# Attention and FFN on one core: the first loads on two queues, and TensorE's order on batch 0 written out

## The chip, the cores and the metric

The kernel runs on one core of one Trainium2 chip. A core has five engines that work side by side, each through its own queue in order: TensorE (PE; its weight loads are shown apart as PEld), VectorE (DVE), ScalarE (ACT), GpSimd (POOL) and SyncE (SP). Transfers are issued from SP, ACT and POOL and carried out by 16 DMA engines. The metric is the device time of one execution in microseconds (us); lower is better.

## The reference

The input is q, k and v, each 8 batches x 12 heads x 448 positions x 64. Every head computes

```
scores = q k^T / 8
attn   = max(scores, 0)^2 / 448
x      = attn v
```

There is no softmax: a ReLU and a square stand in its place. The heads are laid side by side to x of 8 x 448 x 768, and then

```
xn  = (x - mean) / sqrt(var + 1e-6) * g_ln
out = x + max(xn W1, 0) W2        # W1 768 x 3072, W2 3072 x 768
```

All inputs and the output are in fp32; the kernel multiplies in bf16.

## The kernel before, in words

Work goes batch by batch. A batch's 12 heads make three blocks of four heads (`NPER = 3`), numbered n = 0, 1, 2 for batch 0, n = 3, 4, 5 for batch 1, and so on. The 448 positions are cut into 7 pieces of 64 (`J = 7`). For a block:

- `att_T` (transposes, L481) turns q and k so that the head dimension lies on partitions. TensorE transposes into PSUM, and copies (L361 on ACT, L363 on DVE; one helper `copy`, L359) put the result into `qkT`. A block has 56 transposes, 28 of q and 28 of k. From batch 2 on, DMA transposes do this.
- `att_QK(n, s)` (L559) makes the scores of one piece of k against all of q: 4 matmuls into one of three PSUM slots ("slots"). A ReLU with the scale (L568 on ACT, L570 on DVE) writes bf16 to SBUF and frees the slot; a square in place follows (L585 on DVE, L583 on ACT).
- `att_AV(n, s)` (L623) multiplies with v and sums over the seven pieces into two PSUM banks (`f_banks`, for batch 0 alone). After s = 6 the block's part of x, already turned, is copied to `xT_all`, one copy for each half.

When x of a batch is there, `mean_part` (L687, L689, batch 0 alone) or `center` sums over d_model with a matmul against a constant 1/768; DVE subtracts it (L837), ACT or DVE multiplies with g_ln (L826, L828), and the FFN starts: `ffn_1_first` (eight matmuls without a use of their result at L880, then L885) for the first three columns of 128 of W1 on batch 0, `ffn_1` (L902) for the others, evacuated with a ReLU (L918, L920), and `ffn_2` (L959), whose output is scaled and added to x on DVE (L973) and stored. While TensorE runs a batch's FFN, the attention of the next batch is put between its matmuls. 1/std is applied only at that last step, from `bn_stats` of x.

The order is set in three ways. Each engine's queue is in order. What goes onto the queues is decided when the program is built, by a planner (`Order`, L41): each operation has the engines that may do it, a cost on each, its dependencies and a key; the planner keeps a clock for each engine and always commits the operation that can start first, and for one with a choice of engines the one that would end it first. `OVER` (L47) says how much of an instruction overlaps with the next of its queue. And TensorE's pieces come from lists. For batch 0 a loop (L1191) takes from two lists, `av_stream` (transposes of blocks 1 and 2, A.V pieces, mean parts) and `qk_stream` (scores, the transposes of block 3, one score piece of block 3), whichever the planner's clocks let start first. Later `greedy` (L1106, batch 1) and `segment` (L1068) mix FFN and attention in the same manner.

The first loads are written apart (`load_first`, L337): q and k of block 0 come in fp32 through SP's queue, in three transfers (`FIRST`, L335: q whole, k's columns 0 to 2, k's columns 3 to 6), and each is cast to bf16 by DVE or ACT. All others are cast by the DMA itself and issued from POOL (`load`, L316), at most eight in flight, in the order of lines 1163 to 1177: block 1, v, block 2, block 3, then W1 in parts among the rest of batch 1, then W2. The first transposes take the pieces of `FIRST` one by one: q and k's first three columns, then (`att_T(0, 1)`) k's last four; the scores of s < 3 need only the first two pieces.

The copies of block 3's transposes (L523, `pn == 0`, one for q and one for k) are put to the planner as soon as their transposes are. `held_relu` holds back the ReLU of block 3's first score until batch 0's x is copied out (L571 to L579).

Of the kernel before, what the change touches and what calls it, by code (L numbers as in the profile page):

```python
# [40 lines left out]
class Order:  # L41
# [5 lines left out]
    OVER = {"PE": 0.0, "ACT": 80.0, "DVE": 80.0, "POOL": 0.0, "SP": 0.0}  # L47
# [152 lines left out]
def kernel(  # L200
# [31 lines left out]
    N_FILL = 8  # L232
    N_O = 2
# [57 lines left out]
    nc.scalar.activation(warm, eps_sb, Act.Sqrt)  # L291
# [43 lines left out]
    FIRST = ((0, 0, J), (1, 0, 3), (1, 3, J))  # L335

    def load_first():  # L337

        raw = {}
        ops["qk_ld", 0, 0] = []  # L340
        for i, (t, j0, j1) in enumerate(FIRST):
            cols = slice(j0 * D, j1 * D)

            def emit(eng, i=i, t=t, cols=cols):
                if i == 0:
                    stage[0] = big(STAGE[0], None, t=2, r=H // 2, c=S)
                    f = big_pool.tile([P, BIG // 2], fp32, tag=TURNED[1])
                    raw[0] = f[:, :4 * S].rearrange("p (t r c) -> p t r c", t=2, r=2)
                rows = (q, k)[t][0].rearrange("h (p j) d -> (h p) (j d)", j=J).rearrange(
                    "(pr r) c -> r pr c", r=P)  # L350
                nc.sync.dma_start(raw[0][:, t, :, cols], rows[:, 0::NPER, cols])
            ld = R.add("SP", 480.0, emit, [], key=float(i), load=(2 * P, (55.0, 43.0, 110.0)[i]))

            def cast(eng, t=t, cols=cols):
                copy(eng, stage[0][:, t, 0::NPER, cols], raw[0][:, t, :, cols])
            ops["qk_ld", 0, 0].append(
                R.add(("DVE", "ACT"), (100.0 + 67.0 * (j1 - j0), 200.0 + 107.0 * (j1 - j0)), cast, [ld], key=-3.0))
# [107 lines left out]

    def at_use(last):
        at_ring.pop(0)
        at_ring.append(last)
# [3 lines left out]
    def att_T(n, part=0):  # L472
# [17 lines left out]
        if b == 0:  # L490
            evs = ops.setdefault(("T", n), [])
            pieces = list(enumerate(FIRST if n == 0 else ((0, 0, J), (1, 0, J))))
            for i, (t, j0, j1) in pieces[2 * part:2 * part + 2]:
# [26 lines left out]
        if pn == 0:  # L520
            ev = None
            for t in range(2):
                ev = R.add(("DVE", "ACT"), (620.0, 940.0), lambda eng, t=t: copy(  # L523
                    eng, qkT[b][:, t, pn::NPER, :], st[0][:, t].rearrange("p (j c) -> p j c", c=P)), [op, ev], key=0.01 * n - 0.008)
# [6 lines left out]
    def qk_dep(n, s):  # L531
        b, pn = divmod(n, NPER)
        if ("T", n) in ops:
            if n == 0 and s >= FIRST[1][2]:
                return ops["T", n] if len(ops["T", n]) > 2 else None
            return ops["T", n][:2]
# [724 lines left out]
```

## Time and profile before

| What | Value |
|---|---|
| Five runs | 541.92 to 542.89 us, median 542.13 |
| The profiled execution | 542.89 us, of which the span from first to last instruction is 541.03 |
| TensorE busy | 527.7 us, 98% of the span |
| VectorE, ScalarE, GpSimd busy | 285.3, 228.6, 112.6 us |
| TensorE idle before its first instruction | 5.01 us |
| First score matmul, first ReLU, first square | 6.86, 7.50, 8.44 us |
| Last square of batch 0 ends; first FFN matmul (L885) | 26.12; 30.04 us |
| Moved by DMA | 51.83 MB, mean 96 GB/s; about 200 GB/s in the first 60 us |

Times in a view count from the span's start. In the timeline a line gives the start, the busy time of a run of equal instructions, the engine, the source line, the operation and its tiles; in brackets is the idle time before it and what ended it. Instructions of one engine overlap: the next starts before the record of the last ends, so what an operation costs in a full queue is the distance between starts, not its duration. The view of waits gives, for an engine and line, what it waited for, with total, times and longest. The chain of waits follows back from the last instruction what released each step. "PE" times are partly modelled, since matmuls are pipelined.

### The profile page before, as it was taken

Reading aid. Unit: us, or ns where it says so; the run is one execution under the profiler, and the core shown is the slowest. Engines: PE = TensorE matmul, PEld = TensorE weight load, DVE = VectorE, ACT = ScalarE, POOL = GpSimd, SP = SyncE. Lnnn points to the kernel's source line nnn. Section 1 sums busy time; section 2 is a strip of 40 time slices with the busy share of each in tenths; the row PEclk is TensorE's granted clock in tenths of the full one; section 3 lists DMA queues with packets and bytes.
Section 4 is the critical chain, followed back from the end, with each engine's and each line's share of the span. In section 5 each row is a group of like instructions: output and inputs, shape, how many; then the busy total and the mean of one; then the engine's idle time right before and its main releaser. Section 6 shows DMA issues by size and latency. Waiting matters only on the chain.

```text
span 541.0 us, 9859 instructions
## 1 busy us (share of the span) xinstructions
PE 527.7 (98%) x4200; PEld 285.3 (53%) x4200; DVE 285.3 (53%) x486; ACT 228.6 (42%) x376; POOL 112.6 (21%) x129
## 2 busy tenths in 40 slices
PE   4899999999999999999999999999999999999996
PEld 3444455555554455555555455554555555555564
DVE  5979647238764566835366446752456535530011
ACT  5977612125325642556124653265422654144200
POOL 6410600131360124311061121600220102100000
PEclk9999999999999999999999999999999999999999
DMA  9999999996299104980189502993023100510022
GB/s 196 196 190 192 206 171 162 170 133 132 70 159 157 34 1 90 193 119 1 31 107 187 95 1 48 162 150 43 2 59 74 29 1 1 99 48 1 1 58 59
DMA packets 141400, 51.83 MB, mean 96 GB/s; under 512 B 121254, under 2 KB 137132, under 8 KB 141356
## 3 DMA queue, kind: packets, MB, share of 16 engines
q0 software_dynamic: 81072, 25.50, 43.8%
q1 hardware_dynamic: 55804, 14.88, 19.8%
q10 hardware_dynamic: 4480, 10.82, 7.2%
q8 instruction: 33, 0.54, 0.4%
q14 instruction: 11, 0.09, 0.1%
HBM read 51.91 MB, written 11.01 MB: 116 GB/s over the span
## 4 chain that ended last, share of the span: by engine, by line
PE 95%; DVE 2%; DMA 2%; POOL 1%; ACT 0%; issue 0%; POOLq 0%; DVEq 0%
PE o_ps L959 41%; PE ps L902 40%; PE sc L559 6%; PE ps L623 6%; DMA v_t<-in_v_dram 2%; DVE a L585 1%; PE ps L885 1%; PE ps L481 0%; DVE a L570 0%; ACT a L568 0%; POOL t L331 0%; PE ps L689 0%; PE slot L798 0%; DVE t L363 0%; ACT a L826 0%
## 5 line engine op out<-in xcount | busy, mean ns | idle before, releaser
L902 PE MATMUL ps<-a,w 128*128 128x448 bf16 x1134 | 220.4, 353 | 0.0
L959 PE MATMUL o_ps<-w,h 128*128 128x384 bf16 x1200 | 199.7, 326 | 0.0
L902 PEld LDWEIGHTS <-w 128*128 128x128 bf16 x1134 | 108.3, 98 | 108.5 <-issue 10.8
L959 PEld LDWEIGHTS <-h 128*128 128x128 bf16 x1200 | 116.1, 98 | 81.5 <-issue 5.5
L918 ACT ACTIVATE h<-ps 128x448 bf16<-128x448 f32 (+1 forms) x162 | 85.2, 527 | 104.3 <-PE ps L902 102.7
L568 ACT ACTIVATE a<-sc 128x896 bf16<-128x896 f32 x101 | 89.6, 922 | 85.9 <-PE sc L559 82.1
L570 DVE TENSOR_SCALAR a<-sc 128x896 bf16<-128x896 f32 x58 | 63.0, 1087 | 103.6 <-PE sc L559 103.5
L585 DVE TENSOR_TENSOR a<-a 128x896 bf16<-128x896 bf16 x158 | 99.3, 665 | 4.0 <-ACT a L568 3.9
L973 DVE SCALAR_TENSOR_TENSOR o_t<-o_ps,r_t,x_all 128x384 f32<-128x384 f32 x56 | 34.4, 615 | 107.4 <-PE o_ps L959 107.1
L718 POOL TENSOR_TENSOR sum_t<-sum_t,xT_all 128x384 f32<-128x384 f32 (+2 forms) x25 | 19.5, 778 | 166.7 <-ACT xT_all L361 148.1
L559 PE MATMUL sc<-t 64*64 64x448 bf16 x672 | 48.0, 361 | 2.4 <-ACT a L568 1.8
L623 PE MATMUL ps<-a,v_t 64*64 64x448 bf16 x636 | 37.4, 351 | 1.4 <-DMA v_t<-in_v_dram 0.5
L716 POOL TENSOR_TENSOR sum_t<-xT_all 128x384 f32<-128x384 bf16 (+2 forms) x13 | 10.2, 788 | 125.5 <-DVE a L585 97.2
L826 ACT ACTIVATE a<-a,g_sb 128x448 bf16<-128x448 bf16 x38 | 22.3, 656 | 25.8 <-DVE a L819 24.8
L361 ACT CAST xT_all<-ps 128x128 bf16<-128x128 f32 (+3 forms) x40 | 22.2, 560 | 25.2 <-DVE xT_all L363 13.2
L559 PEld LDWEIGHTS <-t 64*64 64x64 bf16 x672 | 17.7, 106 | 24.4 <-issue 19.1
L623 PEld LDWEIGHTS <-v_t 64*64 64x64 bf16 x672 | 19.8, 107 | 16.4 <-issue 4.6
L399 POOL DMA_DIRECT2D t<-in_q_dram x12 | 19.3, 1771 | 24.3 <-DMA t<-t 23.0
L959 PE MATMUL o_ps<-w,t 128*128 128x384 bf16 x144 | 23.9, 326 | 0.0
L399 POOL DMA_DIRECT2D t<-in_k_dram x12 | 23.7, 2525 | 0.0
L819 DVE TENSOR_TENSOR a<-xT_all,sum_t 128x768 bf16<-128x768 bf16 (+1 forms) x24 | 19.4, 852 | 6.7 <-ACT sum_t L811 6.5
L383 POOL DMA_DIRECT2D v_t<-in_v_dram x16 | 17.1, 1440 | 19.1 <-DMA w<-in_moe_w_ch_dram 17.6
(54 smaller groups left out, 187.7 us busy)
## 6 DMA issues: line engine op xcount, KB each, us to landing
out_dram<-o_t ACTq DMA_DIRECT2D x54, 192.0 KB, 2.7
v_t<-in_v_dram POOLq DMA_DIRECT2D x16, 336.0 KB, 15.5
w<-in_moe_w_ch_dram POOLq DMA_DIRECT2D x4, 1152.0 KB, 40.5
t<-in_q_dram POOLq DMA_DIRECT2D x12, 336.0 KB, 7.2
t<-in_k_dram POOLq DMA_DIRECT2D x12, 336.0 KB, 10.6
w<-in_moe_w_ch_dram POOLq DMA_DIRECT2D x4, 768.0 KB, 19.3
w<-in_moe_w_ch_dram POOLq DMA_DIRECT2D x1, 1536.0 KB, 29.3
t<-in_q_dram POOLq DMA_DIRECT2D x5, 224.0 KB, 10.2
```

Of the source, the lines that this page charges most:

```text
L361: nc.scalar.copy(o, i)
L399: nc.gpsimd.dma_start(stage[b][half * T:(half + 1) * T, t].rearrange("p j (h d) -> p j h d", d=D), src[b, half * 6:half * 6 + 6].rearrange ...
L559: nc.tensor.matmul(sc[rows_of(half), r, :S], qkT[b][rows_of(r), 1, s * NPER + pn, rows_of(half)], qT[:, :, pn, rows_of(half)], start=True, ...
L568: nc.scalar.activation(attn[n, s], st[0][:, :, :S], Act.Relu, scale=rc2)
L570: nc.vector.tensor_scalar(attn[n, s], st[0][:, :, :S], rc2, 0.0, op0=Alu.mult, op1=Alu.max)
L585: nc.vector.tensor_mul(attn[n, s], attn[n, s], attn[n, s])
L623: nc.tensor.matmul(av_st[n][half][rows_of(hh)], vt[b][rows_of(half), 2 * pn + hh, s * D:(s + 1) * D], attn[n, s][rows_of(half), hh, :], st ...
L826: nc.scalar.mul(o, o, g_sb[:, ki:ki + 1])
L902: nc.tensor.matmul(st[0], w1[:, ki, ni * P:(ni + 1) * P], xc[b][:, ki, :], start=(i == 0), stop=(i == K1 - 1))
L918: nc.scalar.activation(o, st[0][:, c], Act.Relu)
L959: nc.tensor.matmul(o_st["ps"], stat(ki), w2[:, ki, j * hd:(j + 1) * hd], start=(ki == 0), stop=(ki == K2 - 1))
L973: nc.vector.scalar_tensor_tensor(o_st[u, m][:, j * hd:(j + 1) * hd], ps, rstd[b][:, ri:ri + 1], xm[u, m][:, j * hd:(j + 1) * hd], op0=Alu. ...
```

## The change

The first k is loaded in one transfer from ACT's queue, at the same time as q in one transfer from SP's. Both are cast, transposed and copied in two pieces each (columns 0 to 3 and 4 to 6 of q, 0 to 2 and 3 to 6 of k). So that k's issue stands first on ACT, the activation that loads ACT's table (`warm`) now follows it. TensorE's order on batch 0 is a string of 49 letters, "a" for the next of `av_stream` and "q" for the next of `qk_stream`; `qk_stream` now ends with three score pieces of block 3, of which the string takes none (it has 22 q: 21 scores of batch 0 and block 3's transposes). The copies of block 3's transposes are held until batch 0's x is copied out, as the ReLU was. The planner's overlaps become 112 ns for ACT and 85 for DVE, from 80 for both, and the price of the subtraction 620 in place of 560.

```diff
-    OVER = {"PE": 0.0, "ACT": 80.0, "DVE": 80.0, "POOL": 0.0, "SP": 0.0}
+    OVER = {"PE": 0.0, "ACT": 112.0, "DVE": 85.0, "POOL": 0.0, "SP": 0.0}
...
+    FIRST_ORDER = "aqqqaqqqqqaqaqqaaaaqaqaqaqaaqqaqqqaaaqaaqaaaaaaaa"
...
-    nc.scalar.activation(warm, eps_sb, Act.Sqrt)
...
-    FIRST = ((0, 0, J), (1, 0, 3), (1, 3, J))
+    FIRST = ((0, 0, 4), (0, 4, J), (1, 0, 3), (1, 3, J))
+    LAST = len(FIRST) - 1
+    K_NEAR = FIRST[LAST][1]
 
     def load_first():
 
-        raw = {}
+        f = big_pool.tile([P, BIG // 2], fp32, tag=TURNED[1])
+        raw = f[:, :4 * S].rearrange("p (t r c) -> p t r c", t=2, r=2)
+        stage[0] = big(STAGE[0], None, t=2, r=H // 2, c=S)
+        ld = []
+        for t, src in enumerate((q, k)):
+            def emit(eng, t=t, src=src):
+                rows = src[0].rearrange("h (p j) d -> (h p) (j d)", j=J).rearrange("(pr r) c -> r pr c", r=P)
+                (nc.sync if t == 0 else nc.scalar).dma_start(raw[:, t], rows[:, 0::NPER, :])
+            ld.append(Op("SP" if t == 0 else "ACT", 480.0, emit, [], 0.0, (2 * P, 68.0)))
+            R.commit(ld[t], ld[t].engs[0], 700.0)
         ops["qk_ld", 0, 0] = []
-        for i, (t, j0, j1) in enumerate(FIRST):
+        for t, j0, j1 in FIRST:
             cols = slice(j0 * D, j1 * D)
...
-                nc.sync.dma_start(raw[0][:, t, :, cols], rows[:, 0::NPER, cols])
-            ld = R.add("SP", 480.0, emit, [], key=float(i), load=(2 * P, (55.0, 43.0, 110.0)[i]))
...
+    def wait_for_x(ev):
+
+        if ("x", NPER - 1) in ops:
+            ev.after.append(ops["x", NPER - 1])
+            R.wait.append(ev)
+        else:
+            held_relu.append(ev)
...
-            for i, (t, j0, j1) in pieces[2 * part:2 * part + 2]:
+            for i, (t, j0, j1) in pieces[LAST:] if part else pieces[:LAST if n == 0 else 2]:
...
-                ev = R.add(("DVE", "ACT"), (620.0, 940.0), lambda eng, t=t: copy(
-                    eng, qkT[b][:, t, pn::NPER, :], st[0][:, t].rearrange("p (j c) -> p j c", c=P)), [op, ev], key=0.01 * n - 0.008)
+                ev = Op(("DVE", "ACT"), (620.0, 940.0), lambda eng, t=t: copy(
+                    eng, qkT[b][:, t, pn::NPER, :], st[0][:, t].rearrange("p (j c) -> p j c", c=P)), [op, ev], 0.01 * n - 0.008)
+                wait_for_x(ev)
...
-                s1 = R.add("DVE", 560.0, sub_k, [op], key=-2.0)
+                s1 = R.add("DVE", 620.0, sub_k, [op], key=-2.0)
...
         load_first()
+        nc.scalar.activation(warm, eps_sb, Act.Sqrt)
...
-        qk_stream += [("T", NPER)] + qks(NPER, 0, 1)
+        qk_stream += [("T", NPER)] + qks(NPER, 0, 3)
         att_T(0)
         means = 0
-        while av_stream:
-            R.until(R.free["PE"])
-            tA, tQ = (start_of(piece_deps(*st[0])) if st else FAR for st in (av_stream, qk_stream))
-            if R.ahead(min(tA, tQ)):
-                continue
-            st = av_stream if tA <= tQ + 50.0 else qk_stream
-            p = st.pop(0)
+        for c in FIRST_ORDER:
+            p = (av_stream if c == "a" else qk_stream).pop(0)
             PIECE[p[0]](*p[1:])
```

On the built programs this gives: ACT has k's transfer, the table load, `warm`, the cast of q's columns 0 to 3, ten ReLUs, an x copy, seven ReLUs, an x copy, two ReLUs, an x copy, the copy of g_ln, and then one of the held copies ahead of the gains. DVE has the other three casts, the four pieces' copies, then squares; its held copy stands after its last x copy and before the subtractions. TensorE has all 56 transposes of block 0, three scores, the 56 of block 1, five scores (the fifth of block 1), and then A.V and scores in turn. Block 3's transposes stay before the end of batch 0; its first score moves behind the first FFN columns (L885). In batch 1, too, some ReLUs and squares change engine, and FFN and attention pieces alternate a little differently.

## The prediction

> **What bounds the kernel now.** I read the table of stages first, cut where TensorE's work changes kind; its columns are length, then busy time and instruction count of PE, PEld, DVE, ACT, POOL, then clock, DMA share, GB/s.
>
> ```profile
> 0.00:5.01 5.01, 0.00 (x1) 0.00 (x1) 0.91 (x4) 1.49 (x2) 4.27 (x12) 1.00 0.61 185
> 5.01:28.67 23.66, 19.57 (x405) 11.27 (x406) 20.32 (x36) 18.90 (x26) 11.74 (x17) 1.00 1.26 199
> 28.67:30.04 1.37, 1.19 (x8) 0.59 (x6) 1.37 (x3) 1.09 (x3) 0.42 (x1) 1.00 1.48 110
> 30.04:62.66 32.62, 32.62 (x386) 15.78 (x386) 25.40 (x39) 23.16 (x34) 11.13 (x10) 1.00 1.20 198
> 62.66:536.98 474.32, 474.29 (x3404) 257.65 (x3402) 236.74 (x406) 183.97 (x314) 85.02 (x93) 1.00 0.66 83
> 536.98:541.04 4.06, 0.00 (x0) 0.00 (x0) 0.62 (x1) 0.00 (x0) 0.00 (x0) 0.81 0.18 48
> ```
>
> From 30.04 us, where the first FFN matmul starts (L885), TensorE is busy to the end of its work. So the time is: start of L885, plus the TensorE work still to be done, plus a tail of 4.06. Only 30.04 us can shrink. The chain of waits from 23.5 to 31 us names what sets it:
>
> ```profile
> 24.52 1.61 DVE a L585 x3
> 26.13 0.04 issue
> 26.17 0.57 PE ps L623 x8
> 26.75 0.15 PE ps L687
> 26.90 0.86 PE ps L689 x4
> 27.76 0.31 PE sc L559 x4
> 28.07 0.50 PE ps L689 x2
> ```
>
> VectorE's squares of batch 0 (L585) come last; then the last A.V product, the evacuation of x, the mean (L689), the centering. The waits of ScalarE and VectorE from about 5 to 30 us (total, times, longest) say where they lose time:
>
> ```profile
> ACT a L568 <- PE sc L559: 2.2, 4, 0.7
> DVE t L363 <- DMA f<-in_q_dram: 3.3, 1, 3.3
> DVE a L585 <- ACT a L568: 0.4, 2, 0.2
> ```
>
> ScalarE's 2.2 us are four waits of its ReLUs for scores: 0.69 before 7.50, 0.67 before 10.70, 0.71 before 13.94, 0.16 before 28.13 (timeline of ScalarE). VectorE hardly waits: after its first square at 8.44 it is nearly full.
>
> **What the skill says.** "DMA: Bandwidth & Descriptors", Issuing engines are not separate DMA queues: transfers from several engines share 16 DMA engines and interleave, so a second issuer saves issue time alone. The trace agrees as far as it goes: q's first half megabyte moved at 360 GB/s (2.6 to 3.9 us) and k's at 343 (3.9 to 5.2), one queue at that. "TensorE: Matmul & The Clock Gate", Part 1: the first 3.4 us or so of matmuls run at half clock. Here 40 transposes took 1.28 us at 5.01 (32 ns each) and 53 took 1.01 at 16.96 (19 each); it agrees. "ScalarE: Activation LUTs", What ACT_TABLE_LOAD costs: an activation with immediates costs 186 ns + 0.833 ns an element; L361 on 448 took 0.55, the formula gives 0.56.
>
> **The change, part by part.** Prices, as distances between starts in a full queue: square 0.535 (four from 18.69 to 20.83), PSUM copy or x cast on VectorE 0.535, ReLU on VectorE 1.00 (20.83 to 21.83), ReLU on ScalarE 0.81 (six from 16.76 to 21.61), x cast there 0.415.
>
> *Loads.* Now SP issues q at 0.74 and k in two parts at 1.27 and 1.76; with 3.6, 3.6 and 3.9 us to landing they are there at 4.34, 4.9 and 5.66. After, q leaves SP and k ScalarE at about 0.74. Bytes and engines are the same, so I let both land near the end: 917 KB at the plateau of about 400 GB/s (slices of the DMA view between 2.8 and 3.6 us: 335 to 442) from 2.6 us, plus 0.4 from last data to landing (4.34 against 3.9): about 5.3. Bounds: 4.3 (two queues double the rate) and 5.7 (no gain). Behind k's issue on ScalarE stand the table load (1.28) and `warm` (0.20): from 1.2 to 2.7 us, where ScalarE has nothing else until its first cast; free. On SP only the gains' load follows, now earlier by two issues of 0.46; free. POOL's own load queue starts at about 4.6 as now.
>
> *Casts and copies in pieces.* In the built order ScalarE casts q's four columns: 186 + 0.833 x 512 = 0.61 (skill's formula; trace: none). VectorE casts k's three, k's four, q's three, 0.43 or less each, overlapped: about 1.1. TensorE then does all 56 transposes before the first score: 5.3 + 0.65 = 5.95, plus 56 x 0.032 = 1.79, makes 7.75. q's second piece is cast by 6.4, when the first 16 transposes end at 6.46; no hole. The first score now starts at 6.86: **0.89 us later**. First ReLU 8.39 (now 7.50), first square 9.34 (now 8.44). Four copies on VectorE cost 2 x 0.42 + 2 x 0.35 in place of three, all before 8.4; hidden.
>
> *The fixed list.* It puts three scores behind the first transposes, then batch 0's second transposes, then QK(0,3) to (0,6) and QK(1,0) **ahead of AV(0,0)**. Now AV stands first and blocks TensorE until v lands (wait 0.53 at 12.77), which is the 0.71 hole before 13.94; the 0.67 hole before 10.70 is the second transposes (8.40 to 10.28). With ReLUs running 8.39 to 10.9, those transposes (k landed at 9.39) end at 10.5, so the hole shrinks to about 0.1. QK(1,0) needs only a free slot at 12.9, so its ReLU starts about 13.6 (now 13.94). ScalarE has made up more than its late start.
>
> *VectorE's sum.* From the first square up to the end of the last: now 20 squares, 3 ReLUs, 4 copies, 1 x cast = 10.70 + 3.00 + 2.14 + 0.54 = 16.38 in 17.60 us (8.44 to 26.04), 1.2 of it slips, largely caused by ScalarE's holes. After, in the built order: 21 squares, 2 ReLUs, 4 copies, 2 casts = 11.24 + 2.00 + 2.14 + 1.08 = 16.46. I replayed the list: each ReLU is there before VectorE reaches its square, by 0.1 to 0.9. I take a slip of 0.4; bounds 0 and 1.2. So 9.34 + 16.46 + 0.4 = 26.20, against 26.04: a wash, late start and smoother queue.
>
> *Held copies.* The turning copies of batch 1's first block stand in VectorE's queue at 26.04, two of 0.535, ahead of the last x cast. Held until x, one goes behind that cast and one to ScalarE. QK(3,0), 0.31 in front of the last mean pair, moves behind the first FFN. Last square ends 26.28; A.V 0.05 + 0.38; x cast 26.76 to 27.38; mean 27.43 to 27.98 (0.55); subtraction 28.09 after 0.11. Now 28.67: **0.58 earlier**. On VectorE the held copy ends about 27.9, before the subtraction; on ScalarE its copy (186 + 0.833 x 896 = 0.93) ends by 28.3, before the first gain needs it at 28.7. If x slipped on ScalarE, this copy would delay the gain by up to 0.4.
>
> *The rest.* QK(3,0) comes back after L885, 4 of the 12 scores that take 0.69 there: +0.19 (bound 0.31). The other new ReLU and square placements come from the planner's overlap constants (112 and 85 in place of 80; the 0.62 squares start 0.535 apart, an overlap of 0.085); they stay under TensorE: 25.4 of 32.6 us busy on VectorE, 23.2 on ScalarE. Weight loads land as now; the built order asks for FFN column 8, the tight one (landing 42.4, used at 42.8), only after more attention, about 44.7. Sum: -0.58 + 0.19 = -0.39.
>
> The profiled execution took 542.89 us with a span of 541.03, so 1.86 outside; its new time would be 542.5. It is the slowest of the five; their median 542.13 is 0.76 lower, so I forecast **541.7**.
>
> **The rivals.** A measurement of this kernel tells about 0.2% (1.08 us) from no change.
>
> *A, it all falls well.* If q and k land at 4.6, only 0.3 gets through, since the second block's k lands at 9.39 and its transposes follow. With no slip, 0.4 more: -0.39 - 0.7 = -1.1, 541.0. For it: the replay finds no wait; against: the shared DMA engines and 1.2 of slip now.
>
> *B, the late start is not made up.* VectorE's slip stays 1.2: +0.8, so +0.4, 542.5. For: every square queues behind ScalarE as before. Against: two of the three holes have a cause that the list removes.
>
> *C, slower.* In batch 1's attention (30 to 62.7 us) an FFN bank's evacuation stands on ScalarE behind two ReLUs (2 x 0.81 + 0.54 = 2.16 us), where TensorE has a column (1.24) and a score pair (0.50) to do before it needs the bank: 1.74. That counts once the ReLUs start no earlier than the matmuls end; then 0.42 each, for five columns 2.1, less 0.39: 543.8. For it: the built order has several pairs of ReLUs between evacuations, and batch 1 has one score less in hand. Against: no wait there now, both engines with a quarter of the time free, and the scores before a column usually lead it.
>
> **How the numbers follow.** Forecast 0.57 (541.1 to 542.2), A 0.19, B 0.15, C 0.09. A lies about the bound of -0.2% (541.05) and mostly beyond it: 0.15, with 0.05 for the forecast's lower edge, makes faster 0.20. C and a last 0.01 of B make slower 0.10. The rest, 0.70, is no change that can be told. Range 540.7 to 542.9: it leaves out C and the far half of A, about a tenth at each end.
>
> **What would show it.** Right: first score at about 7.7; both loads landed near 5.3; ScalarE's waits for scores between 9 and 26 us under 0.5; no copy of a turned block between the last square and the last x cast; L885 at about 29.5. Wrong: a landing under 4.7 or over 5.8, L885 before 29 or after 30.3, or any TensorE wait after it.

## The result, and the profile after

| | before | after |
|---|---|---|
| Median of all timed runs | 542.36 us (80 runs) | 543.74 us (43 runs) |
| After / before, 95% interval | | 1.0021 (1.0016 to 1.0026) |
| Profiled execution, and its span | 542.89, 541.03 us | 544.01, 542.24 us |
| First score, first square | 6.86, 8.44 us | 8.89, 10.47 us |
| Last square of batch 0 ends | 26.12 us | 26.99 us |
| First FFN matmul | 30.04 us | 30.71 us |

The changed kernel is slower by 0.21%, about 1.1 to 1.4 us, where 541.7 us (540.7 to 542.9) had been forecast. Numbers of lines are those of the changed kernel here (an experiment's view has the numbers of its own kernel, which differ by a few): scores L570, squares L594, A.V L632, mean L698, copies L363 (ScalarE) and L365 (VectorE), subtraction L846, gains L835, first FFN columns L894.

The table of stages of the changed kernel, cut at the same events as before (TensorE's start, first subtraction, first FFN matmul, 0.35 us behind the start of batch 1's mean, end of TensorE's work); columns are length, then busy time and count of PE, PEld, DVE, ACT, POOL, then clock, DMA share, GB/s.

```profile
0.00:6.21 6.21, 0.00 (x0) 0.00 (x0) 0.56 (x4) 2.10 (x3) 5.47 (x14) 1.00 0.73 184
6.21:29.34 23.13, 18.54 (x401) 11.84 (x402) 19.94 (x38) 17.87 (x24) 10.96 (x15) 1.00 1.26 199
29.34:30.71 1.37, 1.19 (x8) 0.59 (x6) 1.37 (x3) 1.01 (x3) 0.00 (x0) 1.00 1.51 109
30.71:63.51 32.80, 32.80 (x390) 16.07 (x390) 24.61 (x37) 24.17 (x37) 12.07 (x10) 1.00 1.19 196
63.51:538.10 474.59, 474.56 (x3405) 257.70 (x3402) 233.90 (x402) 186.97 (x318) 84.07 (x91) 1.00 0.63 83
538.10:542.24 4.14, 0.00 (x0) 0.00 (x0) 0.62 (x1) 0.00 (x0) 0.00 (x0) 0.86 0.18 48
```

TensorE starts 1.20 us later (6.21 against 5.01). The second stage is shorter than before (23.13 against 23.66), so about half of that is won back. From 30.71 us on TensorE is full again, but the last three stages are longer than before by 0.18 (32.80 against 32.62, one score more), 0.27 (474.59 against 474.32) and 0.08.

The waits of ScalarE and of VectorE from 5 to 31 us (total, times, longest):

```profile
ACT a L579 <- PE sc L570: 3.4, 1, 3.4
ACT t L363 <- DMA f<-in_q_dram: 2.8, 1, 2.8
```

```profile
DVE t L365 <- DMA f<-in_k_dram: 4.8, 1, 4.8
DVE a L594 <- ACT a L579: 1.3, 1, 1.3
```

Before, ScalarE's ReLUs waited four times for scores, 2.2 us in all. Now they wait once, ahead of the very first. After that neither the ReLUs nor the squares wait: in this execution the list did what the prediction said of it. The one wait of 3.4 us isn't to be set against the 2.2, since before the change ScalarE spent most of that time waiting too, ahead of a copy (4.1 us). What counts is that the first ReLU starts at 9.53 in place of 7.50.

The chain of waits between 26 and 31 us (the pauses of 0.02 to 0.04 us that the view lists as "issue" are left out):

```profile
26.35 1.07 PE ps L632 x14
27.43 0.15 PE ps L696
27.58 0.88 PE ps L698 x4
28.48 0.17 ACT g_sb L703
28.70 0.55 PE ps L698 x2
...
29.34 0.63 DVE a L846
30.00 0.68 ACT a L835
30.71 1.29 PE ps L894 x6
```

Between the last A.V product and the last pair of mean matmuls stand the transpose of g_ln (L696), the first four mean matmuls, and the copy of g_ln out of PSUM (L703). The copy of x, which the prediction took for the last step there, isn't in the chain: VectorE's ended at 28.12, 0.58 us before that pair began.

How the start went is in the timelines of before and after, first TensorE and VectorE before (in brackets the idle time ahead and what ended it):

```profile
5.01 1.28 PE L481 MATMUL ps<-identity,t 64*64 64x64 bf16 x40 [5.01 <-DVE t L363]
6.86 0.59 PE L559 MATMUL sc<-t 64*64 64x448 bf16 x4 [0.57 <-ACT t L361]
```

```profile
4.33 1.03 DVE L363 CAST t<-f 128x896 bf16<-128x896 f32 x2 [3.29 <-DMA f<-in_q_dram]
8.44 0.62 DVE L585 TENSOR_TENSOR a<-a 128x896 bf16<-128x896 bf16 x1
```

and after, TensorE, VectorE and ScalarE:

```profile
6.21 0.64 PE L491 MATMUL ps<-identity,t 64*64 64x64 bf16 x16 [6.21 <-ACT t L363]
7.16 1.27 PE L491 MATMUL ps<-identity,t 64*64 64x64 bf16 x40 [0.31 <-DVE t L365]
8.89 1.33 PE L570 MATMUL sc<-t 64*64 64x448 bf16 x12 [0.46 <-DVE t L365]
```

```profile
5.88 1.23 DVE L365 CAST t<-f 128x384 bf16<-128x384 f32 x3 [4.84 <-DMA f<-in_k_dram]
7.73 1.43 DVE L365 COPY t<-ps 128x512 bf16<-128x512 bf16 x4 [0.63 <-PE ps L491]
10.47 0.62 DVE L594 TENSOR_TENSOR a<-a 128x896 bf16<-128x896 bf16 x1 [1.31 <-ACT a L579]
```

```profile
5.54 0.62 ACT L363 CAST t<-f 128x512 bf16<-128x512 f32 x1 [2.79 <-DMA f<-in_q_dram]
```

Three things lie between the load and the first square. q lands at 5.5 instead of 4.3. VectorE casts q's second piece only after both pieces of k, which lands at 5.85, so TensorE waits 0.31 us between its first 16 transposes and the other 40. And after the last transpose VectorE still has to make the copy that the first score needs: 0.46 us more. The chain of waits up to the first score (pauses again left out) begins with k's load, not with q's, and goes through VectorE's three casts:

```profile
0.74 5.11 DMA f<-in_k_dram
5.88 1.24 DVE t L365 x3
7.16 1.29 PE ps L491 x21
8.47 0.37 DVE t L365
8.89 0.61 PE sc L570 x4
```

### The profile page after: what moved, and what is told of

It is laid out like the page before. It is cut to its first block, busy times and chain, and to the rows that moved or that the text cites. A ratio compares the mean times of both kernels' runs of the same rounds, so it can differ in the third digit from the quotient of the medians.

```text
span 542.2 us, 9867 instructions
## 1 busy us (share of the span) xinstructions
PE 527.1 (97%) x4200; PEld 286.2 (53%) x4200; DVE 281.0 (52%) x482; ACT 232.1 (43%) x382; POOL 112.6 (21%) x129
## 4 chain that ended last, share of the span: by engine, by line
PE 95%; DVE 1%; ACT 1%; DMA 1%; issue 1%; ACTq 0%; DVEq 0%
PE o_ps L968 41%; PE ps L911 40%; PE sc L570 6%; PE ps L632 6%; ACT a L579 1%; DMA f<-in_k_dram 1%; PE ps L491 1%; PE ps L894 1%; DVE a L594 1%; DVE t L365 0%; PE ps L698 0%; PE slot L807 0%; ACT xT_all L363 0%; DVE a L581 0%; ACT a L835 0%
## 5 line engine op out<-in xcount | busy, mean ns | idle before, releaser
L927 ACT ACTIVATE h<-ps 128x448 bf16<-128x448 f32 (+1 forms) x169 | 89.5, 530 | 103.4 <-PE ps L911 100.8
L579 ACT ACTIVATE a<-sc 128x896 bf16<-128x896 f32 x103 | 91.1, 924 | 87.4 <-PE sc L570 85.2
L581 DVE TENSOR_SCALAR a<-sc 128x896 bf16<-128x896 f32 x56 | 60.9, 1088 | 108.6 <-PE sc L570 108.4
L594 DVE TENSOR_TENSOR a<-a 128x896 bf16<-128x896 bf16 x159 | 99.8, 669 | 3.7 <-ACT a L579 3.2
L570 PE MATMUL sc<-t 64*64 64x448 bf16 x672 | 47.9, 362 | 2.4 <-ACT a L579 1.7
L632 PE MATMUL ps<-a,v_t 64*64 64x448 bf16 x636 | 36.7, 350 | 1.2 <-ACT xT_all L363 0.7
L835 ACT ACTIVATE a<-a,g_sb 128x448 bf16<-128x448 bf16 x38 | 22.2, 656 | 25.9 <-DVE a L828 24.8
L363 ACT CAST xT_all<-ps 128x768 bf16<-128x768 f32 (+3 forms) x39 | 22.2, 573 | 23.3 <-PE ps L632 15.2
L570 PEld LDWEIGHTS <-t 64*64 64x64 bf16 x672 | 17.6, 106 | 24.9 <-issue 19.6
L632 PEld LDWEIGHTS <-v_t 64*64 64x64 bf16 x672 | 20.2, 107 | 14.5 <-issue 4.2
L385 POOL DMA_DIRECT2D v_t<-in_v_dram x16 | 17.9, 1494 | 17.5 <-DMA w<-in_moe_w_ch_dram 9.6
```

The lines of the kernel that those rows point to most:

```text
L363: nc.scalar.copy(o, i)
L570: nc.tensor.matmul(sc[rows_of(half), r, :S], qkT[b][rows_of(r), 1, s * NPER + pn, rows_of(half)], qT[:, :, pn, rows_of(half)], start=True, ...
L579: nc.scalar.activation(attn[n, s], st[0][:, :, :S], Act.Relu, scale=rc2)
L581: nc.vector.tensor_scalar(attn[n, s], st[0][:, :, :S], rc2, 0.0, op0=Alu.mult, op1=Alu.max)
L594: nc.vector.tensor_mul(attn[n, s], attn[n, s], attn[n, s])
L632: nc.tensor.matmul(av_st[n][half][rows_of(hh)], vt[b][rows_of(half), 2 * pn + hh, s * D:(s + 1) * D], attn[n, s][rows_of(half), hh, :], st ...
```

## The experiments

The theory after the result: *the late start* does the harm. The first square comes 2.03 us later, VectorE's queue is full from there to the last square, and so the delay arrives at the FFN but for what the list saves. The rival: the list, the held copies or the planner's figures (overlaps and price) cost something themselves. The tables collect what was read from each run; each ratio is to runs of the kernel before that were taken beside it. The last two columns of the second table are the two stretches from the first square to the first FFN matmul. "Slip" is what a stretch of VectorE's queue takes beyond the sum of its instructions, a "hole" is idle time within a queue.

| Kernel | median, us | ratio to before (95%) | span of the profile |
|---|---|---|---|
| e1 loads as before | 542.47 | 1.0004 (0.9994 to 1.0013) | 540.84 |
| e2 loads alone | 544.49 | 1.0046 (1.0033 to 1.0058) | 542.62 |
| e3 copies not held | 543.61 | 1.0027 (1.0017 to 1.0038) | 541.82 |
| e4 mean first | 543.82 | 1.0033 (1.0020 to 1.0045) | 542.37 |
| e5 k behind q | 543.15 | 1.0017 (1.0008 to 1.0026) | 541.08 |
| e6 score first | 543.02 | 1.0006 (0.9994 to 1.0019) | 541.49 |
| e7 mean and gains first | 543.08 | 1.0014 (1.0006 to 1.0022) | 541.61 |
| e8 all three | 542.34 | 0.9994 (0.9984 to 1.0004) | 540.47 |
| e11 transposes later | 544.60 | 1.0029 (1.0018 to 1.0041) | 543.11 |
| e12 overlaps 80 | 544.60 | 1.0030 (1.0016 to 1.0044) | 543.51 |
| e13 k issued late | 543.75 | 1.0023 (1.0014 to 1.0033) | 541.99 |
| e14 x copy earlier | 542.04 | 0.9994 (0.9983 to 1.0005) | 540.17 |

| Kernel | first square | last square ends | first FFN matmul | first to last square | last square to FFN |
|---|---|---|---|---|---|
| before | 8.44 | 26.12 | 30.04 | 17.68 | 3.92 |
| before, e9 | 8.46 | 25.46 | 29.38 | 17.00 | 3.92 |
| before, e10 | 9.69 | 26.64 | 30.56 | 16.94 | 3.92 |
| after | 10.47 | 26.99 | 30.71 | 16.51 | 3.73 |
| e1 | 9.22 | 25.80 | 29.52 | 16.58 | 3.72 |
| e2 | 10.21 | 27.82 | 31.55 | 17.61 | 3.73 |
| e3 | 10.14 | 26.65 | 30.38 | 16.51 | 3.73 |
| e4 | 10.47 | 26.99 | 30.19 | 16.51 | 3.20 |
| e5 | 8.86 | 25.86 | 29.58 | 17.00 | 3.72 |
| e6 | 8.69 | 26.42 | 30.14 | 17.73 | 3.72 |
| e7 | 10.47 | 26.98 | 30.19 | 16.51 | 3.21 |
| e8 | 8.45 | 25.92 | 29.13 | 17.47 | 3.21 |
| e11 | 8.58 | 26.73 | 31.43 | 18.14 | 4.70 |
| e12 | 9.38 | 28.62 | 31.99 | 19.24 | 3.37 |
| e13 | 10.14 | 26.66 | 30.38 | 16.51 | 3.73 |
| e14 | 8.43 | 25.63 | 28.84 | 17.20 | 3.21 |

### The loads, undone and alone

e1 is the changed kernel with the three transfers of before on SyncE's queue, and with their casts; e2 is the kernel before with the changed loads and pieces and nothing else.

```diff
-    FIRST = ((0, 0, 4), (0, 4, J), (1, 0, 3), (1, 3, J))
+    FIRST = ((0, 0, J), (1, 0, 3), (1, 3, J))
...
-                (nc.sync if t == 0 else nc.scalar).dma_start(raw[:, t], rows[:, 0::NPER, :])
+                nc.sync.dma_start(raw[0][:, t, :, cols], rows[:, 0::NPER, cols])
```

> The changed kernel, but with the loads, pieces and table load of the kernel before (three transfers on SyncE's queue, q whole, k in columns 0 to 2 and 3 to 6); the written-out list, the held copies and the planner's figures stay. Theory (the late start does the harm: the first square came 2.03 us later and VectorE's queue, full from there on, carries it to the last square): q lands at about 4.3, the first score comes at 7.0 to 7.6 in place of 8.89, the first square at 8.8 to 9.1 in place of 10.47. Not all of that gets through, since the second block's k then lands later again (about 9.4 in place of 8.55) and its transposes stand ahead of the fourth score: VectorE's slip grows from 0 to about 0.8. Last square ends at about 26.2 in place of 26.99, first FFN matmul at 29.9 in place of 30.71, span about 541.4 (540.9 to 541.8), that is 0.8 us under the changed kernel. Rival (the list, the held copies or the planner's figures do the harm): the span stays within 0.3 us of the changed kernel's 542.24, whatever the start does.

> The kernel before with one part of the change alone: k in one transfer on ScalarE's queue beside q, casts and copies in pieces, the table load behind k's issue. TensorE's order comes from the planner's loop, copies are not held, planner's figures as before. Theory (late start): first square at about 10.5 as in the changed kernel, against 8.44; VectorE's queue up to the last square is here 21 squares, 2 ReLUs, 4 copies and 4 x casts, 17.5 us, so the last square ends at about 28.0 to 28.6 (26.12 before), the first FFN matmul comes at 31.4 to 32.0 (30.04), and the span is 1.4 to 2 us over that of the kernel before, about 542.7. Rival (the start is hidden behind other waits of the old order, such as the second block's landing): span within 0.5 us of before, 541.0 to 541.5.

Undoing the loads takes 1.40 us off the span and brings the time back to that of before. The first square comes 1.25 us earlier and 1.19 of it reach the last square: the slip of 0.8 that the theory had allowed for, from the second block's landing, didn't come (16.58 against 16.51). It is a little later than expected, 9.22, because the list puts all 56 transposes ahead of the first score. The loads alone cost 0.46% against before, as the theory said (span 542.62 for 542.7). With them at 1.0046 and the whole change at 1.0021, the rest of the change is worth about 0.25% beside the late loads: the rival falls. But beside the loads of before the rest gains nothing that can be told (e1: 0.9994 to 1.0013), so its gain can't simply be added to another start.

### Which part of the loads: the second queue

```diff
-                (nc.sync if t == 0 else nc.scalar).dma_start(raw[:, t], rows[:, 0::NPER, :])
+                nc.sync.dma_start(raw[:, t], rows[:, 0::NPER, :])
```

> The changed kernel, but k's one transfer is issued on SyncE's queue behind q's instead of on ScalarE's; casts and copies stay in the same four pieces, the list stays. Theory (the two queues share the same DMA engines, so that q, needed first, comes with k instead of before it): q lands at about 4.4 in place of 5.52, k at about 5.6; TensorE starts at about 5.1, and only the second half of its first 56 transposes waits for k: first score at about 7.9 in place of 8.89, first square at about 9.5 in place of 10.47, and the span is 0.8 to 1.0 us under the changed kernel's 542.24, near 541.3. Rival (it is the pieces and the place of the casts that make the start late, whichever queue): first score at 8.6 or later, span 542.0 or more.

In the source the pieces stay and only the queue changes. The rows of issues of the changed kernel, then of this one (the last number is us from issue to landing):

```profile
f<-in_q_dram SPq DMA_DIRECT2D x1, 448.0 KB, 4.8
f<-in_k_dram ACTq DMA_DIRECT2D x1, 448.0 KB, 5.1
```

```profile
f<-in_q_dram SPq DMA_DIRECT2D x1, 448.0 KB, 3.4
f<-in_k_dram SPq DMA_DIRECT2D x1, 448.0 KB, 4.1
```

k, issued half a microsecond later, lands at about 5.35 and so earlier than when it went beside q, and q lands 1.4 us earlier. The first score comes at 7.27 and the first square at 8.86, better than expected. The span, 541.08, meets the 541.3; over all runs the median is 0.6 us under that of the changed kernel, and this kernel varies more from run to run (542.65 to 545.77), so that the two ratios (1.0017 and 1.0021) can't be told apart. The rival in its plain form, a late start whichever queue is used, falls: with the same pieces the start is 1.6 us earlier. But the place of the casts did not stay. With other landing times the planner gave q's second piece to ScalarE, which cast it at 4.19 beside VectorE's cast of the first, ahead of k; in the changed kernel it stands behind k's two casts. So e5 changes the queue and the order of the casts at once.

Is it the sharing, or a second queue that is slow? e13 keeps ScalarE's queue but puts the table load first again.

```diff
+        nc.scalar.activation(warm, eps_sb, Act.Sqrt)
         load_first()
-        nc.scalar.activation(warm, eps_sb, Act.Sqrt)
```

> The changed kernel with ScalarE's table load put back ahead of k's issue, so that k still goes through ScalarE's queue but 1.5 us later (2.2 instead of 0.74). If the delay of q comes from sharing the DMA engines with k, q lands again within 3.8 us of its issue (4.8 in the changed kernel), ScalarE's cast of it starts at about 4.4 to 4.6 in place of 5.54, and k lands at 6.2 to 6.6; the first score, which waits for k, then comes at 9.2 to 9.6 in place of 8.89 and the span is 0.3 to 0.7 over 542.24. If the second queue itself slows both (its set-up, whichever comes first), q still takes 4.5 us or more.

The premise didn't hold: k's issue ran at 0.91, during the table load, not at 2.2. But its first packets came at 3.39 in place of 2.58 all the same (packet times of the trace), and that is enough to see something. The DMA view between 2.5 and 4.25 us gives the packets of each queue (q1 is SyncE's, q10 ScalarE's): first the changed kernel, then e13, then e5.

```profile
q1 hardware_dynamic: 166, 0.30, 53.2%
q10 hardware_dynamic: 132, 0.24, 38.3%
```

```profile
q1 hardware_dynamic: 245, 0.41, 61.9%
q10 hardware_dynamic: 119, 0.21, 31.4%
```

```profile
q1 hardware_dynamic: 377, 0.65, 98.0%
```

The queues take from one supply. In the changed kernel q has 166 packets in this time because k has 132; in e5 one queue moves 377 in it. q lands 4.0 us after its issue in e13 (4.8 in the changed kernel, 3.4 in e5), between the two marks set beforehand (3.8 and 4.5) and with the same second queue: the more of k's packets are in flight the later it comes. This is what the Trainium skill says in "DMA: Bandwidth & Descriptors", Issuing engines are not separate DMA queues. The total in these 1.75 us was 0.53 to 0.58 MB in the five profiles with two queues issued together, and 0.58 to 0.65 MB in the ten with one.

The end is hardly better in e13, since the casts wait for k again (TensorE pauses 0.77 us after its first 16 transposes): first square 10.14, and 543.75 us. q came 0.79 us earlier than in the changed kernel, the first score only 0.34. In all six profiles with this order of casts (after, e2, e3, e4, e7, e13) the first score follows k's landing by 2.88 to 3.04 us; in e5 it follows by 1.92. So of e5's 1.62 us at the first score 0.50 is k's earlier landing, and 1.12 is a shorter way from there, with q cast and transposed ahead of k and one of the four copies on ScalarE. How much of the 1.12 the earlier landing of q brings and how much the other place of casts and copies isn't shown: no run moved the casts alone.

### The held copies, and what the mean waits for

e3 gives the copies of block 3's transposes to the planner at once, as before the change.

```diff
-                wait_for_x(ev)
+                R.wait.append(ev)
```

> The changed kernel, but the two copies of block 3's transposes go to the planner as soon as they can, as before; in the built order one stands on ScalarE ahead of batch 0's last x copies and one on VectorE right behind the last square. Theory: the last mean pair does not wait for the x copy but for the first four mean matmuls and the copy of g_ln behind them (it started at 28.70 though x was copied out by 28.12), so the copies have 0.6 us of room; ScalarE's copy ends at about 27.3, before A.V ends at 27.43. First FFN matmul at 30.7 within 0.15, span within 0.2 us of the changed kernel's 542.24. Rival, as the prediction had it (the copies stand in the way of x): subtraction 0.5 us later, span about 542.8.

From first square to first FFN matmul it takes 20.24 us, to the hundredth what the changed kernel takes; all of its 0.34 us at the FFN is an earlier start (10.14). Here ScalarE makes one of the copies ahead of both x copies, and the chain still runs past it (pauses left out):

```profile
27.24 0.88 PE ps L698 x4
28.14 0.17 ACT g_sb L703
28.36 0.55 PE ps L698 x2
```

So holding the copies brings nothing in this order of TensorE: the prediction's largest gain, 0.58 us, rested on the wrong last wait. e4 goes for the right one. It puts the transpose of g_ln and the first four mean matmuls ahead of the last five A.V pieces, and block 3's transposes behind the last mean pair.

```diff
-        av_stream += [("M", n) for n in range(NPER)]
+        av_stream[-5:-5] = [("M", 0), ("M", 1)]
+        av_stream.append(("M", 2))
...
-    FIRST_ORDER = "aqqqaqqqqqaqaqqaaaaqaqaqaqaaqqaqqqaaaqaaqaaaaaaaa"
+    FIRST_ORDER = "aqqqaqqqqqaqaqqaaaaqaqaqaqaaqqaqqqaaaqaaaaaaaaaaq"
-    N_FILL = 8
+    N_FILL = 2
```

> The changed kernel with TensorE's order at the end of batch 0 altered: the transpose of g_ln and the first four mean matmuls go ahead of the last five A.V pieces, and block 3's transposes go from there to behind the last mean pair, where they take the place of six of the eight filling matmuls. Theory (the last mean pair waits on the first four and the g_ln copy): the last pair then starts when x is copied out, at about 28.1 in place of 28.70, subtraction at 28.75 in place of 29.34, first FFN matmul at 30.1 in place of 30.71, span about 541.7, 0.55 us under the changed kernel. Rival (the last x copy or A.V sets it): the four mean matmuls, 0.93 us, delay the last A.V pieces, and the first FFN matmul comes at 30.7 or later.

The first FFN matmul comes at 30.19 as expected, 0.52 us earlier; but the span doesn't follow. TensorE and ScalarE of this kernel:

```profile
30.19 1.29 PE L894 MATMUL ps<-a,w 128*128 128x448 bf16 x6
32.11 2.43 PE L894 MATMUL ps<-a,w 128*128 128x448 bf16 x12 [0.62 <-ACT a L835]
```

```profile
30.61 0.88 ACT L363 COPY t<-ps 128x896 bf16<-128x896 bf16 x1
31.39 0.67 ACT L835 ACTIVATE a<-a,g_sb 128x448 bf16<-128x448 bf16 x1
```

A held copy, 0.88 us, got between two gains, and TensorE waited 0.62 us for the second. In e7 the copies wait for the last gain.

```diff
+        for ev in held_copies:
+            ev.after.append(ops["xc", 0])
+            R.wait.append(ev)
```

> The kernel of the run with the mean matmuls first, except that the two held copies of block 3's transposes now wait for the last multiplication with g_ln. There one copy stood on ScalarE between two of these multiplications, and TensorE waited 0.62 us for the fourth, in the middle of its first FFN columns. Theory: that wait goes, the first FFN matmul stays at about 30.2, and the span is 541.7, 0.55 us under the changed kernel. Rival (the copies then come too late for block 3's first score at 34): the wait moves to that score, span 542.2 or more.

```profile
30.19 3.56 PE L895 MATMUL ps<-a,w 128*128 128x448 bf16 x18
```

The 18 matmuls run through, the span is 541.61 for the expected 541.7, and the median is 0.66 us under that of the changed kernel (the intervals of the two ratios overlap). That the first mean matmuls and the g_ln copy set the mean is thus shown by moving them. Block 3's transposes moved with them, but they had not been in the way: in the changed kernel the last four A.V matmuls began at 27.04, 0.05 us behind the last square.

### An early start and the list together

e6 is e1 with the first score ahead of k's last transposes and four scores ahead of block 1's; e8 adds the edits of e7.

```diff
-    FIRST_ORDER = "aqqqaqqqqqaqaqqaaaa...
+    FIRST_ORDER = "qaqqqqaqqqaqaqqaaaa...
```

> The kernel of the run with the loads of before, with the beginning of the list altered: the first score ahead of the transposes of k's last four columns, and four scores instead of three ahead of block 1's transposes. Theory: the list put all 56 transposes before the first score, which with the loads of before still cost 0.78 us at the first square (9.22 against 8.44 before); now the first score comes at 6.9, the first square at 8.45, and with VectorE's queue of 16.4 us and a slip of 0.1 to 0.5 the last square ends at about 25.1 (25.80), the first FFN matmul comes at 28.9 (29.52), span about 540.2 (540.84). Rival (block 1's landing sets the pace up to there): the holes come back in ScalarE's queue and the span stays within 0.2 us of 540.84.

> All together: the loads of before, the first score ahead of k's last transposes, four scores ahead of block 1's transposes, the first mean matmuls ahead of the last A.V pieces, and the held copies behind the multiplications with g_ln. If the gains add up: last square ends at about 25.1, first FFN matmul at about 28.3 (30.04 before the change, 30.71 after), span about 539.6, 1.4 us under the kernel before and 2.6 under the changed one. If they don't (a transfer of W1 or v sets the pace instead): first FFN matmul at 29 or later, or a wait of TensorE for weights behind it, span 540.3 or more.

Neither meets its expectation: 541.49 for 540.2, and 540.47 for 539.6. The start is early (8.69 and 8.45), but the stretch to the last square grows to 17.7 and 17.5 us. TensorE, then VectorE, of e8:

```profile
17.13 0.98 PE L493 MATMUL ps<-identity,t 64*64 64x64 bf16 x51 [1.28 <-DVE xT_all L366]
```

```profile
18.60 0.61 DVE L596 TENSOR_TENSOR a<-a 128x896 bf16<-128x896 bf16 x1
20.00 0.62 DVE L596 TENSOR_TENSOR a<-a 128x896 bf16<-128x896 bf16 x1 [0.79 <-ACT a L581]
```

Block 2's transposes wait 1.28 us for the banks that hold block 0's x, the scores behind them are late, and VectorE has a hole of 0.79. In the changed kernel the same transposes wait 0.49 us, and VectorE, which runs later there, has no hole; so the smooth queue of the changed kernel seems in part bought by its late start. e11 tried to fill the hole with one more score ahead of these transposes, and e12 the same with the planner's old overlaps.

```diff
-...aaaaqaqaqaqaa...
+...aaaaqaqqaqaaa...
```

> The kernel with all three edits, with one score moved ahead of block 2's transposes in the list. There TensorE waited 1.2 us at these transposes for VectorE's copy of block 0's x, the scores behind them came late, and VectorE's queue had a hole of 0.79 us at 19.2. Theory: the score ahead of them keeps ScalarE busy, the hole goes, the first FFN matmul comes at 28.4 (29.13), span about 539.7 (540.47), which would be 0.8 us under a typical span of the kernel before. Rival (the hole moves to another wait, as ScalarE's ReLUs and VectorE's squares are both nearly full): first FFN matmul at 28.9 or later, span 540.2 or more.

> The kernel before this one with the planner's overlaps at 80 and 80 again, as before the change, in place of 112 and 85. The changed kernel lost 0.15 us more than before at one FFN column of batch 1, at 66.9 us. Theory (the planner's figures moved ReLUs and squares ahead of that column's evacuation): with 80 the stretch from the first FFN matmul to that of the second product, 67.21 us with the new figures, is 67.05 and the span is 0.15 under that kernel's. Rival (that slip comes from the moved score or from chance): 67.2 again, or more where the old figures bring holes elsewhere.

Both failed. The next score after the transposes now belongs to block 2, so it waits 1.06 us for their copies, and the hole moves there: the rival of e11 was right. Not all of e11's 2.30 us at the first FFN matmul is the hole, though: 1.49 lie behind the last square, where TensorE's clock had fallen to half (last section), and k's last columns landed 0.94 us later than in e8. In e12 k's last columns also landed late (cast at 7.80). On the planner's figures e12 gives half an answer: from batch 1's mean to the second product it takes 34.61 us, where e11 takes 34.76. The other profiles agree: 34.62 in the four with the old figures (before, e2, e9, e10), 34.76 in all eleven with the new ones. So the new figures cost 0.15 us there. But the stretch ahead of it grew in e12 (32.70 against 32.61), and whether the old figures would pay in all isn't settled.

e14 instead takes the wait itself away, in e8: block 0's x copies go one place earlier in both queues.

```diff
-                ev = R.add(("DVE", "ACT"), (620.0, 560.0), evac, [op], key=-1.0)
+                ev = R.add(("DVE", "ACT"), (620.0, 560.0), evac, [ops["av", n, J - 3] if n == 0 else op], key=-1.0)
```

> The kernel with all three edits, but with the copies of block 0's x one ReLU earlier in ScalarE's queue and one square earlier in VectorE's, since block 2's transposes waited 1.2 us for them there and left a hole of 0.79 us in VectorE's queue. Theory: the transposes come 0.5 us earlier, most of the hole goes, but VectorE then also makes both copies of block 2's transposes (0.54 more), so that the first FFN matmul comes at about 28.8 (29.13) and the span is 540.1 (540.47). Rival (both engines are full and the hole only moves): first FFN matmul at 29.1 or later.

28.84 and 540.17, as expected. Its median, 542.04, is the lowest of all kernels, 1.7 us under the changed kernel. Against the kernel before, its interval (0.9983 to 1.0005) takes in 1: no version was found that is measurably better than that one.

### The kernel before, twice more

> The kernel before, unchanged, profiled in another execution. The profile that the prediction worked from had a span of 541.03 us where most executions of that kernel have 540.2 to 540.6. Theory: that execution lost 0.5 to 0.8 us in the stage before the first FFN matmul, by a later landing or by a larger slip of VectorE's queue (1.2 us there), so a typical one has a first square at about 8.4 again, a slip of 0.4 to 0.7, and its first FFN matmul at 29.2 to 29.6; the changed kernel then has less slip to win back than the prediction counted. Rival: the difference lies elsewhere (in batch 1 or the tail), and the first FFN matmul stands at 30.0 as before.

> The kernel before, unchanged, profiled once more, for the spread between executions of the start of its VectorE queue. Both theories as for the second profile of it: first FFN matmul at 29.2 to 29.6 if the first profile was a late one, at 30.0 if the difference lies elsewhere.

The first FFN matmul was at 29.38 and at 30.56: the profile of before was neither typical nor extreme. In e10 the second transfer of k landed 6.3 us after its issue (3.9 in the first profile, 4.0 in e9), which VectorE's timeline shows as a wait:

```profile
8.12 0.43 DVE L363 CAST t<-f 128x512 bf16<-128x512 f32 x1 [1.52 <-DMA f<-in_k_dram]
```

The first profile's 17.68 us from first to last square had 0.7 us of slip that neither of the others has. This changes what the list can win: on an execution like these two 0.5 us in that stretch (16.51 against 17.0), not 1.2. And even the 16.51 stands beside a late start: with first squares at 8.69, 8.45 and 8.43 the lists of e6, e8 and e14 took 17.73, 17.47 and 17.20 us.

## Why the prediction was wrong

The forecast for the span was -0.39 us, the profiles say +1.20 (what lies outside the span went from 1.86 to 1.77). Term by term:

| Step, as the prediction had it | forecast | measured | off by |
|---|---|---|---|
| Loads, casts, pieces: first square | 9.34 | 10.47 | +1.13 |
| VectorE's queue, first to last square | 16.94 | 16.52 | -0.42 |
| Held copies: last square to subtraction | 1.81 | 2.35 | +0.54 |
| Subtraction to first FFN matmul | 1.37 | 1.37 | 0 |
| QK(3,0) comes back behind it | +0.19 | +0.18 | -0.01 |
| Everything later stays under TensorE | 0 | +0.27 | +0.27 |
| Tail | 0 | +0.08 | +0.08 |
| Sum | -0.39 | +1.20 | +1.59 |

Two steps failed, the start and the held copies; the shorter queue made up for 0.42 us of them.

**The start** is the larger of the two, 1.13 of the 1.59 us. Its direction was right, and e1, e2 and e5 show that it decides the result; the times were wrong, and one term was put at nothing. Of the 1.13 us, 0.26 is the first cast: q landed at 5.52 where 5.3 was taken (5.26 to 5.72 in the five profiles with these loads). 0.43 is the run of 56 transposes, 2.22 us instead of 1.79. The prediction let both loads land at 5.3, and so had q's second piece, behind both casts of k, "cast by 6.4" without a hole; but k landed at 5.85, beyond the bound of 5.7, and the three casts ran from 5.88 to 7.10. And 0.46 is the copies: they were called "hidden" before 8.4, but the one that the first score needs begins only when the last transpose has ended.

**The list** did in this execution what was said of it: the holes are gone, and VectorE took 16.43 us from the start of its first square to the end of the last one's place in the queue, where the sum of instructions gave 16.46. The slip of 0.4 that was added didn't come. That seems in part luck of the late start: e6 and e8, with early starts and nearly this list, took 1.22 and 0.96 us longer for this stretch, and beside the loads of before (e1) the rest of the change gained nothing.

**The held copies** are the step whose reasoning failed: it took the wrong wait for the last one. The prediction put "x cast 26.76 to 27.38" straight ahead of the mean, and took the chain's QK(3,0) and the copies for what was in the way. But TensorE had the transpose of g_ln and four mean matmuls to do after the last A.V product, 0.93 us, and then the last pair waited for the copy of g_ln, which has the mean's PSUM tile. The first profile held the sign: x was out at 27.72, and the pair began at 28.01, right behind the copy of g_ln at 27.96. e3 shows that the copies, where the planner puts them without the hold, cost nothing, e4 and e7 that the mean matmuls cost 0.52. The 0.19 us that this stretch did shorten comes with one A.V piece less behind the last square; e2 has it too (3.73), without held copies.

**The rest** of batch 1 did not stay under TensorE: one column was 0.15 us late at 67 us, in a spot that e12's old overlaps removed, and 0.12 more went near 191 us, which e1, e3 and e4 don't have, e5 and e13 do, and for which no cause was found. (The +0.19 for QK(3,0) does not follow from the figure given with it, since 4 of 12 scores that take 0.69 us make 0.23; it measured 0.18.)

Last, the level. The forecast took 0.76 us off because the profiled execution of before stood that far over its median. The profile of after stands only 0.27 over its own: its runs lie within 543.68 and 544.5, while those of before spread from 541.81 to 544.98. In after, e3 and e13 the way from first square to first FFN matmul is 20.24 us each time. So an execution of before that was late by chance was used as if its lateness would carry over. Of the rivals, B (the late start is not made up) named what happened, but by a slip of VectorE's queue that did not come; the start itself carried it. Of the signs of being wrong that the prediction named, two came: a landing over 5.8 (k's) and the first FFN matmul after 30.3.

## What to carry to other kernels

When two loads are needed one after the other, issue them one after the other: beside each other the first one lands nearly as late as the second (5.52 and 5.85 us here, 4.17 and 5.35 in e5). And keep the casts of the first ahead of those of the second: in e13 q came 0.79 us earlier and bought 0.34, since a cast of q stood behind k's. A chain's last wait has to be read at its last instruction, with all it depends on: an engine that is late because of its own work ahead (four matmuls and a small copy) is not helped by clearing the queue of another. And a sum over a full queue forecasts well (16.46 for 16.43 us), so the care belongs to its start: the order of the first casts and copies, one by one.

## What had not been expected of the hardware

- Two queues issued at the same moment (0.74 us) did not begin together: SyncE's first packets came at 1.85, ScalarE's at 2.58 (1.85 to 1.87 and 2.46 to 2.87 in the five profiles).
- The last of the three small transfers took 3.9 to 6.3 us from issue to landing in nine profiles with the loads of before, where it is still under way when GpSimd's own loads begin (about 4.6 us). With two queues issued together, both landed 4.5 to 5.3 us after their issue in all five profiles. That such a late transfer is what spreads the runs of before is likely from e10, but was not tried by itself. The runs fit it: the six kernels with k on ScalarE's queue spread by 0.16 to 1.08 us from the fastest to the slowest run, the eight with it on SyncE's queue by 1.01 to 3.17.
- The same cast on VectorE, 128x512 from fp32 to bf16, took 0.41 to 0.71 us in different runs, 0.69 in the changed kernel's; no cause was found.
- TensorE's clock fell inside e11 and e12 alone, to half for 3.41 us each. These are the stretches of 3.41 us before and of the fall, first in e11, then in e12 (columns as in the tables of stages; the third from the end is the clock):

```profile
21.22:24.63 3.41, 1.66 (x28) 0.92 (x30) 3.33 (x6) 3.41 (x6) 1.31 (x3) 1.00 1.30 170
24.63:28.05 3.42, 3.42 (x25) 1.14 (x24) 1.25 (x2) 1.60 (x3) 1.73 (x3) 0.50 1.25 206
```

```profile
17.62:21.03 3.41, 1.53 (x68) 1.28 (x71) 3.41 (x8) 2.24 (x5) 0.77 (x2) 1.00 1.24 205
21.03:24.44 3.41, 3.19 (x37) 1.39 (x33) 2.21 (x5) 3.04 (x4) 1.64 (x2) 0.50 1.34 168
```

  In each the clock fell at the end of a stretch in which TensorE was busy for less than half of the time, 1.66 and 1.53 of 3.41 us, though no single pause there was longer than 1.06 us. If each profile is cut into such stretches from the first rise of its clock on, every later change of the clock while TensorE works lies on a cut, and no other stretch of the 16 profiles is busy for less than 2.07 us (in e6, where the clock stayed full). A single pause of 1.28 us in e8 had no such effect. The half clock has its price: in e11 the first four mean matmuls took 1.67 us in place of 0.93.
- The half clock at TensorE's start lasted longer than the 3.4 us or so that the prediction takes from the Trainium skill and finds to agree. Before, one score matmul took 0.58 us at 7.90 and 0.35 from 10.41 on, 5.4 us behind the first transpose; in the changed kernel the full clock came at 12.03, 5.8 us behind it.
